# Convolving in full 128-row chunks through a DRAM scratch, with VectorE transposes in place of TensorE ones, in a convolution with two MLP layers

## The chip, the cores and the metric

The kernel runs on one core of a Trainium2 chip. The metric is the device time of one execution in microseconds (us). The core's engines are TensorE (PE for its matmuls, PEld for its weight loads), VectorE (DVE), ScalarE (ACT), GpSimd (POOL) and SyncE (SP), which here only issues DMAs. Each engine takes its instructions in program order and waits at the first one whose inputs are not ready.

## The reference, cut to what matters

```
w = softmax(weight, axis=-1)                      # 8 heads x 7 taps
x_pad = concat([zeros(B, 6, 192), x], axis=1)     # x: 2 x 4096 x 192, float32
y[b, s, h*24+g] = sum_k w[h, k] * x_pad[b, s+k, h*24+g]
y = y.reshape(8192, 192)
h = y @ moe_w_in                                  # 192 -> 2048
z = maximum(0.01*h, h) @ moe_w_out                # 2048 -> 192
h = z @ moe2_w_in                                 # 192 -> 2048
P = a0 + a1*h + a2*h^2 + a3*h^3
Q = 1 + |b0|*|h| + |b1|*h^2
out = (P / (Q + 1e-6)) @ moe2_w_out               # 2048 -> 192
```

## The kernel before

The 8192 tokens are cut into 16 blocks of 512. For each block, `prep` makes the convolved x in transposed form (channels on the partitions, 512 tokens along the row), `layer1` runs the first MLP over 16 tiles of 128 hidden units, `middle` splits its result for the next layer, `layer2` runs the second MLP over 16 tiles, and `finish` transposes and stores the result. Every factor is split into a high part of reduced precision and the rest, so a tile costs five 512-column matmuls in `gemm1` and five in `gemm2_hi` and `gemm2_lo`.

`prep` has these steps. `load_x` brings 512 tokens and their six predecessors into `xt` as five overlapping chunks of 109 rows. `conv` is, for each of two halves m of the channels, four matmuls of a banded matrix with the five chunks, each of 103 rows out and 120 columns; in float32 one such matmul leaves two records in the trace. `conv_evac` (ScalarE) copies the bank into `xc`, with a second copy of the last 64 channels for half 1. `trans` turns the chunks with five TensorE transposes for each half, the tokens put into the bank from the far end; `x_hi` (ScalarE) and `x_lo` (VectorE) then read the bank backwards and write `xh` and `xl`, from which `gemm1` reads. All banks that `conv`, `trans` and `gemm1` write come from one pool of four.

The order is written out by a planner. Each group of instructions has a rank, which is the due time of its tile (`t1` for layer 1, `t2` for layer 2) plus an offset for its kind (`OFF`). The planner goes through a modelled time and gives each engine the group that could start soonest, with a small pull (`PULL`) towards low ranks, among the `LOOK` lowest ranks within `WINDOW` of the lowest one left. `LEAD` is how long layer 1 runs alone at the start, `GAP` and `REST` set how far layer 2 follows behind, `STEP` is the planned time of a pair of tiles. A group with two engines named goes to the one that would end sooner. The buffers `work` (13, later 19, of 128x512 float32), `pair` and the banks are handed out in the same pass. Blocks 0 and 1 take turns in layer 1 while the weights still arrive and are split; from there on a block's layer 1 runs beside layer 2 of the block two before it. Before the first convolution, `s_warm` runs 13 matmuls that nothing reads.

Of the kernel before, what the change touches and what calls it, by code (L numbers as in the profile page):

```python
# [28 lines left out]
LOOK = 38  # L29
REST = 4.152  # L30
OFF = {'xfin_add': -25.96, 'xfin_main': -7.7, 'l2_rs': -12.47, 'l2_Q': -48.45, 'l2_lo': 22.42, 'cv_clip': 21.92, 'r_lo': 27.46, 'gemm2_lo': -13.68, 'fin_trans': 97.39, 'cv_abs': -48.47, 'gemm2_hi': -0.01, 'l2_R': -19.09, 'cv_low': -1.23, 'fin_evac': -37.98, 'trans': -11.11, 'mid_swap': -3.6, 'x_hi': 19.65, 'conv': -13.63, 'l2_p3': 0.9, 'r_hi': -31.67, 'x_lo': -0.75, 'fin_rest': -14.96, 'l2_abs': 32.4, 'l2_r': -7.07, 'l1_lo': -12.51, 'l2_D': -21.65, 'cv_bits': 22.1, 'l2_hi': -11.32, 'mid_add': -16.39, 'gemm1': -7.21, 'w_lo': -3.25, 'fin_add': -37.65}
TAIL = 0.239
FIN = 3.219
CV1, CV2, CV3 = 4.19, 18.33, 7.456
EVERY, INPLACE = 2, (1,)
N_WORK = 13
# [135 lines left out]
def conv_leaky_rational_kernel(  # L172
# [295 lines left out]
    def trans(eng, i, m):
        n = blocks[i][2]
# [433 lines left out]
```

## Time and profile before

| what | value |
|---|---|
| median of 3 runs | 1262.86 us (1261.99 to 1263.27) |
| the profiled execution | 1263.62 us |
| its span, first to last instruction | 1261.8 us |
| PE busy | 1235.6 us, 98% |
| ACT busy | 1145.2 us, 91% |
| DVE busy | 1100.1 us, 87% |
| POOL busy | 1033.2 us, 82% |
| mean granted TensorE clock | 0.993 |

Some 1.8 us of the execution lie outside the span. The profiled execution is 0.76 us above the median. The busy time of PE counts each matmul from its start to its modelled end, and matmuls overlap, so a busy PE is measured by how often a new matmul starts and not by its busy share alone.

### The profile page before, as it was taken

To read this page: it belongs to the slowest core of one execution; us is meant where nothing else is said; L and a number is where in the kernel's file an instruction comes from. 1 tells how busy PE (TensorE), PEld (TensorE's weight loads), DVE (VectorE), ACT (ScalarE), POOL (GpSimd) and SP (SyncE) were. 2 spreads that over 40 slices of the span, in tenths; PEclk is the share of its full clock that TensorE was granted. 3 is DMA by queue.
4 is the path that set the end of the run, shared out by engine and by line. 5 is a ranking of instruction groups with operands and counts; after the bars stand their busy time and mean duration, and the time that the engine had idled before them with its cause. 6 is when DMAs were issued, how large, how long until landed. Compare 5 with 4: busy or idle time off the path is not lost.

```text
span 1261.8 us, 17670 instructions
## 1 busy us (share of the span) xinstructions
PE 1235.6 (98%) x5584; PEld 1011.9 (80%) x5584; DVE 1100.1 (87%) x1661; ACT 1145.2 (91%) x2006; POOL 1033.2 (82%) x987
## 2 busy tenths in 40 slices
PE   8999999999999999999999999999999999999986
PEld 6887888888888788888888888888888888888764
DVE  6998989897987979889798888988888889889998
ACT  6999999999998989999898989989999999999996
POOL 2876878888797887969888888887888878788897
PEclk9999999999999999999999999999999999999989
DMA  7650001010000101010010101001010000000000
GB/s 216 181 157 7 1 1 29 1 28 1 14 15 1 28 1 29 1 29 1 1 29 1 29 1 28 1 1 28 1 29 1 13 1 1 13 1 13 1 13 14
DMA packets 70235, 30.25 MB, mean 24 GB/s; under 512 B 52566, under 2 KB 67580, under 8 KB 70140
## 3 DMA queue, kind: packets, MB, share of 16 engines
q1 hardware_dynamic: 68524, 28.91, 9.2%
q8 instruction: 44, 0.72, 0.2%
q14 instruction: 51, 0.42, 0.1%
q10 hardware_dynamic: 1616, 0.21, 0.1%
HBM read 20.70 MB, written 6.30 MB: 21 GB/s over the span
## 4 chain that ended last, share of the span: by engine, by line
PE 84%; ACT 8%; DVE 6%; issue 2%; DMA 1%; POOL 0%; SPq 0%; DVEq 0%; ACTq 0%; POOLq 0%
PE bank L249 43%; PE acc L249 40%; ACT work L240 4%; ACT raw L240 2%; DVE work L246 1%; PE bank L474 1%; DVE xl L243 1%; DVE pair L246 1%; DVE raw L246 1%; DVE bank L246 1%; DVE work L243 1%; DMA xt<-in_x_dram 1%; DVE raw L243 0%; ACT xh L240 0%; DVE pair L243 0%
## 5 line engine op out<-in xcount | busy, mean ns | idle before, releaser
L249 PE MATMUL acc<-pair,wo 128*128 128x512 f32 x2560 | 645.5, 392 | 2.5 <-DVE pair L243 1.2
L249 PEld LDWEIGHTS acc<-pair,wo 128*128 128x128 f32 x2560 | 478.1, 188 | 103.1 <-DVE pair L243 2.3
L240 ACT ACTIVATE work<-work 128x512 f32<-128x512 f32 x512 | 317.9, 630 | 21.4 <-DVE work L246 15.3
L243 POOL TENSOR_TENSOR work<-work,pair 128x512 f32<-128x512 f32 x181 | 234.7, 1298 | 54.3 <-DVE pair L246 49.5
L249 PE MATMUL bank<-xh,wiH 128*128 128x512 f32 x512 | 205.6, 402 | 14.7 <-DVE work L246 10.5
L249 PE MATMUL bank<-xl,wiR 128*128 128x512 f32 x512 | 200.6, 392 | 0.7 <-DVE xl L243 0.7
L249 PE MATMUL bank<-xh,wiL 128*128 128x512 f32 x512 | 200.6, 392 | 0.1
L249 PE MATMUL bank<-xl,wiH 128*128 128x512 f32 x512 | 200.5, 392 | 0.0
L249 PE MATMUL bank<-xh,wiR 128*128 128x512 f32 x512 | 200.4, 391 | 0.0
L243 POOL TENSOR_TENSOR pair<-work,work 128x512 fp32r<-128x512 f32 x122 | 157.8, 1296 | 25.9 <-DVE work L246 10.6
L246 DVE SCALAR_TENSOR_TENSOR work<-work,b_sb,bank 128x512 f32<-128x512 f32 x178 | 132.0, 741 | 45.2 <-ACT work L240 44.1
L246 DVE SCALAR_TENSOR_TENSOR pair<-bank,a_sb,work 128x512 fp32r<-128x512 f32 x177 | 131.4, 745 | 25.7 <-PE acc L249 15.5
L243 POOL TENSOR_TENSOR pair<-work,pair 128x512 fp32r<-128x512 f32 x96 | 125.4, 1307 | 32.0 <-PE acc L249 23.6
L240 ACT ACTIVATE work<-bank,a_sb 128x512 f32<-128x512 f32 x168 | 129.7, 772 | 19.0 <-PE bank L249 17.9
L246 DVE SCALAR_TENSOR_TENSOR work<-bank,a_sb,work 128x512 f32<-128x512 f32 x181 | 134.4, 743 | 12.5 <-POOL work L243 12.0
L249 PEld LDWEIGHTS bank<-xh,wiH 128*128 128x128 f32 x512 | 96.4, 188 | 47.2 <-DVE work L246 17.3
L246 DVE SCALAR_TENSOR_TENSOR bank<-work,a_sb,bank 128x512 f32<-128x512 f32 x168 | 125.4, 749 | 2.2
L240 ACT ACTIVATE raw<-raw 128x512 f32<-128x512 f32 x192 | 119.9, 630 | 8.0 <-DVE raw L246 5.9
L240 ACT ACTIVATE work<-bank,b_sb 128x512 f32<-128x512 f32 x178 | 121.4, 682 | 0.0
L249 PEld LDWEIGHTS bank<-xl,wiR 128*128 128x128 f32 x512 | 96.7, 189 | 21.6 <-DVE xl L243 1.1
L243 DVE TENSOR_TENSOR work<-work,bank 128x512 f32<-128x512 f32 x168 | 113.6, 677 | 0.0
L249 PEld LDWEIGHTS bank<-xl,wiH 128*128 128x128 f32 x512 | 96.7, 189 | 20.8 <-DVE xl L243 0.2
(96 smaller groups left out, 2002.2 us busy)
## 6 DMA issues: line engine op xcount, KB each, us to landing
raw<-in_moe_w_out_dram SPq DMA_DIRECT2D x16, 384.0 KB
xt<-in_x_dram SPq DMA_DIRECT2D x14, 384.0 KB
out_dram<-work SPq DMA_DIRECT2D x67, 64.0 KB
raw<-in_moe_w_in_dram SPq DMA_DIRECT2D x8, 512.0 KB
raw<-in_moe_w_in_dram SPq DMA_DIRECT2D x8, 256.0 KB
work<-work SPq DMA_DIRECT2D x16, 128.0 KB
out_dram<-raw SPq DMA_DIRECT2D x26, 64.0 KB
xt<-in_x_dram SPq DMA_DIRECT2D x18, 72.0 KB
```

The costliest lines, as they stand in the source:

```text
L240: nc.scalar.activation(out=out_, in_=in_, func=func, **k)
L243: (eng or nc.vector).tensor_tensor(out=out_, in0=in0, in1=in1, op=op)
L246: nc.vector.scalar_tensor_tensor(out=out_, in0=in0, scalar=s, in1=in1, op0=op0, op1=op1)
L249: nc.tensor.matmul(out=out_, lhsT=w, rhs=r, start=start, stop=stop)
L474: nc.tensor.transpose(ps[:, c1 - k:c1], xc[0:k, t, m * P:(m + 1) * P], ident[0:k, 0:k])
```

## The change

Blocks 0 and 1 stay as they are. For the other 14 blocks the convolution no longer goes block by block. The tokens from 1024 on are cut into chunks of 122 rows out of 128 rows in, 26 for the rest of the first sequence and 34 for the second, and these are put into 13 groups of four or five chunks. For each group, `load_g` loads one chunk per DMA, `conv_g` convolves it, `evac_g` copies the bank to `xc` without the extra 64 channels, and `put_g` writes the rows to a scratch tensor `y_dram` in DRAM, in token order from the far end, with two DMAs for a full chunk (112 and 10 rows).

For each block, `get_y` then reads the scratch back in eight DMAs of 64 KB (four for each half m), each in runs of 32 channels (128 bytes), so that 32x32 squares lie side by side in a `work` buffer, and `turn_y` transposes the squares on VectorE. `y_hi` (ScalarE or GpSimd) and `y_lo` (GpSimd or VectorE) split the result, now read from SBUF and not from a bank. The warm-up is 8 of the old matmuls and 19 short ones on a buffer that VectorE fills (`s_seed`). The planner's constants are new, among them the offsets in `OFF`.

```
-LEAD = 81.083
-GAP = 10.083
-PREP = 12.338
-WARM = 13
+LEAD = 66.057
+GAP = 6.373
+PREP = 56.276
+AHEAD = 40.0
+WARM = 8
+SHAPES = ((192, 6, 1), (384, 3, 1), (512, 3, 1), (256, 3, 1), (192, 4, 0))
...
-STEP = 4.683
-PULL = 0.003
-WINDOW = 94.713
-LOOK = 38
-REST = 4.152
+STEP = 4.016
+PULL = 0.005
+WINDOW = 193.974
+LOOK = 58
+REST = -0.364
...
-TAIL = 0.239
+TAIL = 5.502
-CV1, CV2, CV3 = 4.19, 18.33, 7.456
+CV1, CV2, CV3 = -20.785, 58.237, 26.634
...
+    CG = P - (K - 1)
...
-    xc = const.tile([CT, NTC, D + R], F32, name="xc")
+    xc = const.tile([CG, NTC, D + R], F32, name="xc")
+    y_dram = nc.dram_tensor("y_dram", (B * S, D), F32, kind="Internal").ap()
...
+    DIRECT = 2
+    groups = []
+    for bi in range(B):
+        t0 = max(blocks[DIRECT][3] - bi * S, 0) if bi == 0 else 0
+        count = -(-(S - t0) // CG)
+        starts = [min(t0 + c * CG, S - CG) for c in range(count)]
+        ng = -(-count // NTC)
+        at = 0
+        for g in range(ng):
+            k = min(NTC, -(-(count - at) // (ng - g)))
+            groups.append((bi, starts[at:at + k], t0 + at * CG))
+            at += k
...
+        t = xh[1][0][0]
+        for cols, count, step in SHAPES:
+            for n in range(count):
+                k = n * step % 4
+                mm(acc[0][1][:, 0:cols], t[:, k * P:(k + 1) * P], t[:, 0:cols], True, True)
...
+    def conv_g(eng, g, m):
+        k = len(groups[g][1])
+        pv = buf[("gps", g, m)][0:CG, 0:k * HC].rearrange("p (t c) -> p t c", t=k)
+        for hh in range(HB):
+            h = m * HB + hh
+            mm(pv[:, :, hh * G:(hh + 1) * G], band[:, h, P - CG:P], xt[g % 2][:, 0:k, h * G:(h + 1) * G], True, True)
...
+        act(xc[:, 0:k, m * HC:(m + 1) * HC], pv, ACTF.Copy)
...
+    def put_g(eng, g):
+        bi, starts, t0 = groups[g]
+        for c, s0 in enumerate(starts):
+            rows = s0 + CG - (t0 + c * CG)
+            r0 = B * S - bi * S - s0 - CG
+            even = rows - rows % 16
+            for a, z in ((0, even), (even, rows)):
+                if z > a:
+                    nc.sync.dma_start(out=y_dram[r0 + a:r0 + z, :], in_=xc[a:z, c, 0:D])
+
+    def get_y(eng, i, m):
+        n, tok0 = blocks[i][2:4]
+        r0 = B * S - tok0 - n
+        for d in range(1 + m):
+            for q in range((P, R)[m] // 32):
+                p0 = 32 * q + R * d
+                src = y_dram[r0:r0 + n, m * P + 32 * q:m * P + 32 * (q + 1)].rearrange("(b r) c -> r b c", r=32)
+                dst = buf[("ym", i, m)][p0:p0 + 32, 0:n].rearrange("r (b c) -> r b c", c=32)
...
+                    nc.sync.dma_start(out=dst, in_=src)
+
+    def turn_y(eng, i, m):
+        n = blocks[i][2]
+        nc.vector.transpose(out=buf[("yt", i, m)][:, 0:n], in_=buf[("ym", i, m)][:, 0:n])
...
+    def group(g):
...
+        on(SP(P * k * D * 4, k), max(base - 50, 8), 2.0, load_g, g, w=[xk], extra=DMA_LAND)
+        for m in range(2):
+            gps = ("gps", g, m)
+            on(PE(HB * 2 * (0.0025 + k * G / 1200.0)), base, 2.0 + 0.01 * m, conv_g, g, m, r=[xk, ("band", m)], w=[gps],
+               take=("bank", gps))
+            on(ACT(t_act(k * HC)), base, 4.0 + 0.01 * m, evac_g, g, m, r=[gps], w=[("xc", m)])
+        on(SP(0, k), base, 6.0, put_g, g, r=[("xc", 0), ("xc", 1), ("xc", 2)], w=[("y", g)], extra=DMA_LAND)
+
+    def fetch(i):
+        n, tok0 = blocks[i][2:4]
+        base = t1[i * NJ] - AHEAD
...
+            on(SP(0, 4), base, 12.0 + m, get_y, i, m, r=yk, w=[ym], take=("work", ym), extra=DMA_LAND + 1.0)
+            on(DVE(t_dve(n)), base, 18.0 + m, turn_y, i, m, r=[ym], w=[yt], take=("work", yt))
...
+            on(ACT(t_act(n, True)) + POOL(t_pool1(n)), base, 20.0 + m, y_hi, i, m, src, r=[yt], w=[("xh", 0, m, p)])
+            on(POOL(t_pool(n)) + DVE(1.2), base, 22.0 + m, y_lo, i, m, src, r=[yt, ("xh", 0, m, p)], w=[("xl", 0, m, p)])
...
     def prep(i):
+        if i >= DIRECT:
+            while made[0] < len(groups) and groups[made[0]][0] * S + groups[made[0]][2] < blocks[i][3] + blocks[i][2]:
+                group(made[0])
+                made[0] += 1
+            fetch(i)
+            return
```

## Rows read from the trace of the kernel before

**Rows 1.** Windows: stretch, us, then busy PE, PEld, DVE, ACT, POOL (instructions), clock, DMA, GB/s

```profile
160.00:1160.00 1000.00, 997.91 (x4559) 823.45 (x4558) 872.90 (x1304) 919.83 (x1604) 837.73 (x786) 1.00 0.05 12
...
1160.00:1261.80 101.80, 83.50 (x326) 63.02 (x324) 92.39 (x138) 87.55 (x148) 84.78 (x77) 0.93 0.05 9
```

**Rows 2.** Waits of PE in 160 to 1160 us, the longest: total us, times, longest

```profile
PE bank L249 <- ACT work L240: 0.8, 2, 0.5
```

**Rows 3.** The chain that ended last, one long piece: start us, length us

```profile
199.28 4.53 PE acc L249 x20
```

**Rows 4.** Groups by line and shape: busy us, mean ns, idle before

```profile
L249 PE MATMUL acc<-pair,wo 128*128 128x512 f32 x2560 | 645.5, 392 | 2.5 <-DVE pair L243 1.2 <-POOL pair L243 1.0
L249 PE MATMUL bank<-xl,wiH 128*128 128x512 f32 x512 | 200.5, 392 | 0.0
L249 PE MATMUL bank<-xt,band 109*103 109x120 f32 x256 | 32.2, 270 | 0.2 <-DMA xt<-in_x_dram 0.2
L474 PE MATMUL bank<-ident,xc 103*128 103x103 f32 x128 | 16.7, 253 | 0.2 <-ACT xc L240 0.2
```

**Rows 5.** Timeline of PE around one `conv` and one `trans`: start us, length us

```profile
1085.20 0.98 PE L249 MATMUL bank<-xt,band 109*103 109x120 f32 x8
1085.94 0.48 PE L249 MATMUL bank<-xh,wiH 128*128 128x512 f32 x1
1086.26 0.39 PE L249 MATMUL bank<-xh,wiL 128*128 128x512 f32 x1
...
1099.39 0.61 PE L474 MATMUL bank<-ident,xc 103*128 103x103 f32 x5
1099.78 1.40 PE L249 MATMUL acc<-pair,wo 128*128 128x512 f32 x5
1101.01 0.39 PE L249 MATMUL bank<-xh,wiH 128*128 128x512 f32 x1
```

**Rows 6.** Groups by line and shape, the other engines' steps of `prep` and their kin

```profile
L240 ACT ACTIVATE xh<-bank 128x512 fp32r<-128x512 f32 x32 | 18.9, 595 | 0.2 <-PE bank L474 0.2
L240 ACT ACTIVATE xc<-bank 103x480 f32<-103x480 f32 x32 | 18.1, 566 | 3.8 <-PE bank L249 3.7
L240 ACT ACTIVATE xc<-bank 103x320 f32<-103x320 f32 x15 | 6.5, 435 | 0.0
L527 POOL TENSOR_SCALAR pair<-work 128x512 fp32r<-128x512 f32 x69 | 44.1, 640 | 20.6 <-ACT work L240 12.9 <-PE acc L249 5.2 <-DVE bank L372 2.3
L243 POOL TENSOR_TENSOR pair<-work,pair 128x512 fp32r<-128x512 f32 x96 | 125.4, 1307 | 32.0 <-PE acc L249 23.6 <-ACT pair L240 1.8 <-DVE work L243 1.5
```

**Rows 7.** VectorE's work on `xl` by source: ns min/median/max, first and last start

```profile
L243 DVE TENSOR_TENSOR xl<-bank,xh x32: 672/680/692, 14.7 to 1105.5; 128x512 fp32r<-128x512 f32 x32
...
L243 DVE TENSOR_TENSOR xl<-work,xh x9: 679/881/1469, 99.6 to 1119.8; 128x512 fp32r<-128x512 f32 x9
L243 DVE TENSOR_TENSOR xl<-raw,xh x7: 692/1476/1785, 257.9 to 1193.1; 128x512 fp32r<-128x512 f32 x7
```

**Rows 8.** The SBUF-to-SBUF transposes of `finish`: ns min/median/max

```profile
L628 DVE STREAM_TRANSPOSE work<-work x9: 659/693/704, 194.8 to 1257.7; 64x512 f32<-64x512 f32 x9
```

**Rows 9.** SP's issues of the 64 KB output stores: ns min/median/max

```profile
L636 SPq DMA_DIRECT2D out_dram<-work x67: 315/488/1806, 193.7 to 1258.5; - x67
```

**Rows 10.** Windows of 1 us: six such stores, then a load of x

```profile
268.00:269.00 1.00, 1.00 (x7) 0.81 (x6) 0.95 (x2) 1.00 (x3) 1.00 (x3) 1.00 0.62 109
...
273.00:274.00 1.00, 1.00 (x6) 0.80 (x6) 1.00 (x3) 0.52 (x1) 0.91 (x1) 1.00 0.77 253
```

**Rows 11.** Timeline of PE at the start

```profile
2.40 8.51 PE L249 MATMUL acc<-qc,ident 128*128 128x256 f32 x26 [2.40 <-POOL ident masks.py:199]
10.74 1.81 PE L249 MATMUL bank<-xt,band 109*103 109x120 f32 x16
```

**Rows 12.** One window of 40 us in the steady stretch

```profile
320.00:360.00 40.00, 39.51 (x178) 32.45 (x177) 37.97 (x58) 38.60 (x67) 32.31 (x31) 1.00 0.10 23
```

**Rows 13.** Waits of PE over the whole span: total us, times, longest

```profile
PE bank L249 <- DVE work L246: 10.5, 10, 3.1
```

More of the change, by code (lines that the diff above doesn't have):

```diff
@@ L19 @@
 SIZES = [512] * 16
-LEAD = 81.083
-GAP = 10.083
-PREP = 12.338
-WARM = 13
+LEAD = 66.057
[4 more added lines that the diff above has]
+SHAPES = ((192, 6, 1), (384, 3, 1), (512, 3, 1), (256, 3, 1), (192, 4, 0))
 WIDE = 256
 FILL = {'conv': 1, 'trans': 1}
-STEP = 4.683
-PULL = 0.003
-WINDOW = 94.713
-LOOK = 38
-REST = 4.152
-OFF = {'xfin_add': -25.96, 'xfin_main': -7.7, 'l2_rs': -12.47, 'l2_Q': -48.45, 'l2_lo': 22.42, 'cv_clip': 21.92, 'r_lo': 27.46, 'gemm2_lo': -13.68, 'fin_trans': 97.39, 'cv_abs': -48.47, 'gemm2_hi': -0.01, 'l2_R': -19.09, 'cv_low': -1.23, 'fin_evac': -37.98, 'trans': -11.11, 'mid_swap': -3.6, 'x_hi': 19.65, 'conv': -13.63, 'l2_p3': 0.9, 'r_hi': -31.67, 'x_lo': -0.75, 'fin_rest': -14.96, 'l2_abs': 32.4, 'l2_r': -7.07, 'l1_lo': -12.51, 'l2_D': -21.65, 'cv_bits': 22.1, 'l2_hi': -11.32, 'mid_add': -16.39, 'gemm1': -7.21, 'w_lo': -3.25, 'fin_add': -37.65}
-TAIL = 0.239
+STEP = 4.016
[3 more added lines that the diff above has]
+REST = -0.364
+OFF = {'xfin_add': 27.93, 'xfin_main': -41.19, 'l2_rs': -6.51, 'l2_Q': -76.54, 'l2_lo': 20.05, 'cv_clip': 21.93, 'r_lo': -1.28, 'gemm2_lo': -4.32, 'fin_trans': 100.9, 'cv_abs': -25.96, 'gemm2_hi': -3.11, 'l2_R': -14.71, 'cv_low': -5.24, 'fin_evac': -75.01, 'trans': -38.96, 'mid_swap': -4.79, 'x_hi': 22.32, 'conv': -29.75, 'l2_p3': 3.44, 'r_hi': 17.48, 'x_lo': 2.67, 'fin_rest': -19.55, 'l2_abs': 22.74, 'l2_r': 2.84, 'l1_lo': -25.06, 'l2_D': -10.01, 'cv_bits': -8.15, 'l2_hi': -1.95, 'mid_add': -112.83, 'gemm1': -4.61, 'w_lo': -48.12, 'fin_add': -69.89, 'load_g': 63.41, 'conv_g': -23.42, 'evac_g': -35.87, 'put_g': 12.36, 'get_y': -27.55, 'turn_y': 19.29, 'y_hi': -15.46, 'y_lo': -20.59}
+TAIL = 5.502
 FIN = 3.219
-CV1, CV2, CV3 = 4.19, 18.33, 7.456
+CV1, CV2, CV3 = -20.785, 58.237, 26.634
 EVERY, INPLACE = 2, (1,)
@@ L336, in s_warm, with s_seed @@
             mm(acc[0][1][:, 0:WIDE], ident, qc[:, 0:WIDE], True, True)
+        t = xh[1][0][0]
[3 more added lines that the diff above has]
+                mm(acc[0][1][:, 0:cols], t[:, k * P:(k + 1) * P], t[:, 0:cols], True, True)
+    def s_seed(eng):
+        nc.vector.tensor_copy(out=xh[1][0][0], in_=qc)
     def s_fill(eng, count):
@@ L442, in zero_x, with load_g, zero_g, evac_g @@
         nc.vector.memset(xt[i % 2][0:K - 1, 0, :], 0.0)
+    def load_g(eng, g):
+        bi, starts, _ = groups[g]
+        t = xt[g % 2]
+        for c, s0 in enumerate(starts):
+            if s0 == 0:
+                load_rows(t, K - 1, c, x[bi, 0:CG, :], CG)
+            else:
+                nc.sync.dma_start(out=t[:, c, :], in_=x[bi, s0 - (K - 1):s0 + CG, :])
+    def zero_g(eng, g):
+        nc.vector.memset(xt[g % 2][0:K - 1, 0, :], 0.0)
+    def conv_g(eng, g, m):
[4 more added lines that the diff above has]
+            mm(pv[:, :, hh * G:(hh + 1) * G], band[:, h, P - CG:P], xt[g % 2][:, 0:k, h * G:(h + 1) * G], True, True)
+    def evac_g(eng, g, m):
+        k = len(groups[g][1])
+        pv = buf[("gps", g, m)][0:CG, 0:k * HC].rearrange("p (t c) -> p t c", t=k)
+        act(xc[:, 0:k, m * HC:(m + 1) * HC], pv, ACTF.Copy)
+    def put_g(eng, g):
+        bi, starts, t0 = groups[g]
+        for c, s0 in enumerate(starts):
+            rows = s0 + CG - (t0 + c * CG)
[12 more added lines that the diff above has]
+                dst = buf[("ym", i, m)][p0:p0 + 32, 0:n].rearrange("r (b c) -> r b c", c=32)
+                with nc.allow_non_contiguous_dma("columns of the convolution"):
+                    nc.sync.dma_start(out=dst, in_=src)
+    def turn_y(eng, i, m):
+        n = blocks[i][2]
+        nc.vector.transpose(out=buf[("yt", i, m)][:, 0:n], in_=buf[("ym", i, m)][:, 0:n])
     def conv_view(t, n):
@@ L459, in conv_evac @@
         ntc = -(-n // CT)
-        act(xc[:, 0:ntc, m * HC:(m + 1) * HC], pv, ACTF.Copy)
+        act(xc[0:CT, 0:ntc, m * HC:(m + 1) * HC], pv, ACTF.Copy)
         if m == 1 and i:
-            act(xc[:, 0:ntc, D:D + R], pv[:, :, HC - R:HC], ACTF.Copy)
+            act(xc[0:CT, 0:ntc, D:D + R], pv[:, :, HC - R:HC], ACTF.Copy)
     def conv_wrap(eng, i):
         pv = conv_view(buf[("cps", i, 1)], blocks[i][2])
-        nc.vector.tensor_copy(out=xc[:, 0:pv.shape[1], D:D + R], in_=pv[:, :, HC - R:HC])
+        nc.vector.tensor_copy(out=xc[0:CT, 0:pv.shape[1], D:D + R], in_=pv[:, :, HC - R:HC])
     def trans(eng, i, m):
@@ L477, in x_hi, with y_hi, y_lo @@
         n = blocks[i][2]
-        act(xh[l][m][i % 2][:, 0:n], src()[:, 0:n])
+        if eng == "POOL":
+            nc.gpsimd.tensor_scalar(out=xh[l][m][i % 2][:, 0:n], in0=src()[:, 0:n], scalar1=1.0, scalar2=0.0,
+                                    op0=ALU.mult, op1=ALU.add)
+        else:
+            act(xh[l][m][i % 2][:, 0:n], src()[:, 0:n])
     def x_lo(eng, l, i, m, src):
         n = blocks[i][2]
-        tt(xl[l][m][i % 2][:, 0:n], src()[:, 0:n], f(xh[l][m][i % 2][:, 0:n]), ALU.subtract)
+        tt(xl[l][m][i % 2][:, 0:n], src()[:, 0:n], f(xh[l][m][i % 2][:, 0:n]), ALU.subtract,
+           nc.gpsimd if eng == "POOL" else nc.vector)
+    def y_hi(eng, i, m, src):
+        x_hi(eng, 0, i, m, src)
+    def y_lo(eng, i, m, src):
+        x_lo(eng, 0, i, m, src)
     def gemm1(eng, l, i, j):
@@ L700, in conv_leaky_rational_kernel @@
     on(SP(0, 2), -60, 0, s_small, r=["tdram"], w=["ab"], extra=DMA_LAND)
-    on(PE(0.6 * WARM), -74, 0, s_warm, r=["ident", "qc"], w=[("acc", 0, 1)])
+    on(DVE(0.4), -83, 0, s_seed, r=["qc"], w=[("xh", 1, 0, 0)])
+    on(PE(0.6 * WARM + 2.2), -74, 0, s_warm, r=["ident", "qc", ("xh", 1, 0, 0)], w=[("acc", 0, 1)])
     on(ACT(0.2), -40, 0, s_abs, r=["ab"], w=["ab"])
@@ L731, in x_keys @@
         return [(t, l, m, i % 2) for t in ("xh", "xl") for m in range(2)]
-    def prep(i):
+    def group(g):
+        bi, starts, _ = groups[g]
+        k, p = len(starts), g % 2
+        first = next(i for i in range(NB) if blocks[i][3] + blocks[i][2] > bi * S + groups[g][2])
+        base = t1[first * NJ] - AHEAD
+        xk = ("xt", p)
+        if starts[0] == 0:
+            on(DVE(0.25), base - 50, 2.0, zero_g, g, w=[xk])
+        on(SP(P * k * D * 4, k), max(base - 50, 8), 2.0, load_g, g, w=[xk], extra=DMA_LAND)
[8 more added lines that the diff above has]
+        base = t1[i * NJ] - AHEAD
+        yk = [("y", g) for g, (bi, starts, t0) in enumerate(groups)
+              if bi * S + t0 < tok0 + n and bi * S + starts[-1] + CG > tok0]
+        for m in range(2):
+            ym, yt = ("ym", i, m), ("yt", i, m)
+            on(SP(0, 4), base, 12.0 + m, get_y, i, m, r=yk, w=[ym], take=("work", ym), extra=DMA_LAND + 1.0)
+            on(DVE(t_dve(n)), base, 18.0 + m, turn_y, i, m, r=[ym], w=[yt], take=("work", yt))
+            src = lambda k=yt, n=n: buf[k][:, 0:n][:, ::-1]
+            p = i % 2
+            on(ACT(t_act(n, True)) + POOL(t_pool1(n)), base, 20.0 + m, y_hi, i, m, src, r=[yt], w=[("xh", 0, m, p)])
+            on(POOL(t_pool(n)) + DVE(1.2), base, 22.0 + m, y_lo, i, m, src, r=[yt, ("xh", 0, m, p)], w=[("xl", 0, m, p)])
+    made = [0]
+    def prep(i):
+        if i >= DIRECT:
[4 more added lines that the diff above has]
+            return
         n = blocks[i][2]
```

## The prediction

> **What bounds the kernel now.** I read the busy windows first, then PE's waits, the chain, and the pace of single matmuls. In the stretch from 160 to 1160 us PE is busy for 997.91 of 1000 us, ACT for 919.8, DVE for 872.9, POOL for 837.7 [rows 1]. A busy PE can still be a stalled one, so the pace decides: 20 matmuls of 512 columns in a row take 4.53 us, 0.2265 us each [rows 3]. The program has 5120 of them: 2560 into `acc`, and five groups of 512 in `gemm1`, of which one is shown [rows 4]. That is 1159.7 us.
>
> A half of `conv` costs PE 0.834 us: its eight records start at 1085.20, the second matmul after them at 1086.26, and one matmul of 0.2265 lies between [rows 5]. A half of `trans` costs 0.488 us: from 1099.39 to 1101.01 there are 1.62 us, five large matmuls take 1.13 of them [rows 5]. So a block costs PE 320 x 0.2265 + 2 x 0.834 + 2 x 0.488 = 75.1 us, and 1000 us hold 13.3 blocks, or 4602 records at 346 a block. The window shows 4559 [rows 1]: PE runs there within 1% of its own pace, and its longest kind of wait sums to 0.8 us [rows 2]. In the middle, PE's work sets the time; the reader is to see that whatever is taken off PE there comes off the end, as long as the other three keep up.
>
> All of PE's work is 1159.7 + 16 x (1.67 + 0.98) = 1202.1 us. The other 59.7 us of the span of 1261.8 are the start, some stalls before 160 us, and the tail, where PE is busy for only 83.5 of 101.8 us while DVE has 92.4 [rows 1].
>
> **The change part by part, on PE.** Fourteen blocks lose `trans`: 28 x 0.488 = 13.7 us. They lose 28 halves of `conv`, 23.4 us, and 13 groups of two halves come in their place. Eight groups have five chunks, 120 columns as now; five have four, 96 columns. If columns count, this is 16 x 0.834 + 10 x 0.667 = 20.0 us, a saving of 3.4. But the band is now 122 columns wide and not 103, and if that width sets the pace, 26 x 0.834 x 122/103 = 25.7 us, a loss of 2.3. The columns that stream are nearest to what the row shows; I take a saving of 2.0 us, inside the two ends and short of the better one. PE in sum: 13.7 + 2.0 = 15.7 us less (11.4 to 17.1).
>
> **The other engines.** ScalarE loses 14 x (2 x 0.566 + 0.435 + 2 x 0.595) = 38.6 us and gains 26 copies of at most 0.566, 14.7 us [rows 6]. `y_hi` adds 28 x 0.64 = 17.9 us, on POOL at the price of its like [rows 6] or on ScalarE, for which I take the same. VectorE loses 28 x 0.68 = 19.0 us of `x_lo` [rows 7] and gains 28 transposes of 0.693 [rows 8], 19.4 us: even. `y_lo` reads two SBUF operands. On POOL its like takes 1.307 us [rows 6], 36.6 us in all; on VectorE the same operation with an SBUF source has medians of 0.881 and 1.476 where a bank as source has 0.680 [rows 7], so 25 to 41 us.
>
> By block, now: ScalarE 919.8/13.3 = 69.2 us, VectorE 65.6, POOL 63.0. Afterwards PE needs 75.1 - 15.7/14 = 74.0 us. With every choice against it, ScalarE has 68.8 us (93%), VectorE 68.6 (93%), POOL 66.9 (90%). In the window from 320 to 360 us PE lost 0.49 us with ScalarE at 96.5% and VectorE at 95% [rows 12]. So the three stay below the load at which PE was seen to wait, by a margin of a few per cent. I price them at nothing; the cover is PE's own work, and without it they cost what the second rival below says.
>
> **The DMAs.** SP issues per block eight fetches, and about nine pieces of `put_g` and four or five loads, where it had three loads; at 0.488 us an issue [rows 9] some 18 more issues are 9 us of a 74 us block. They are hidden as long as `get_y` is issued early (it waits for the landing of `put_g`, and behind it in SP's queue stand output stores, loads of x and, early on, weight pieces). Eight fetches move 512 KB in 128-byte runs. Output stores have such runs too and move 109 GB/s at 0.62 of the DMA engines, where a load of x reaches 253 [rows 10]: 4.7 us a block, of 74. The plan allows a half of `get_y` 2.4 us to issue and 3.3 us to land; four issues of 0.488 and 256 KB at 109 GB/s are 2.0 and 2.4 us. I price this at nothing; if it is late, `turn_y` stands at the head of VectorE's queue, behind it the layer 2 steps that give banks back, and then PE.
>
> A rule of the Trainium skill speaks against this part: "DMA: Bandwidth & Descriptors", Specifications, puts the least transfer for full rate at 512 bytes. The trace agrees in kind (109 against 253 GB/s [rows 10]). If all fetches lay open, 14 x 4.7 = 66 us would be added and the sum would be 1313 us; the third rival takes a part of it.
>
> A second one does: "VectorE: DVE Perf Modes", Rules for kernel authors, sends a 128x128 transpose to TensorE where PSUM will do as destination. Rows bear it out by the engine's own time, 0.488 us for a half on PE [rows 5] against 0.693 on VectorE [rows 8]. By it the old way stays, at 1262.9 us; by what bounds this stretch, PE's 0.488 is dear and VectorE's 0.693 is not.
>
> **Start, end and buffers.** The warm-up before was 8.51 us for 26 records, and the first `conv` stands right behind it, at 10.74 [rows 11]. The new one has 16 such records, 5.2 us, and 5376 columns, 2.4 us at 0.2265 for 512 or twice that at half the clock: 0.9 us less to 1.5 us more. I take nothing for it. Two banks a block are no longer taken for `trans`, four `work` buffers are taken instead: PE's waits for banks in the steady stretch are too small to gain from [rows 2], and I price the buffers with the second rival. The new constants move the start and the end; no row prices them, so I bound them by the tail: nothing to gain, or a part of its 18.3 us of idle PE [rows 1], or a loss of the same size. I take nothing.
>
> **Sum.** Profiled execution 1263.62 (span and 1.8 us around it) - 15.7 = 1247.9 us. It stands 0.76 us above the median of the runs, so 1247 us as a median.
>
> **The rivals.**
>
> 1. *The forecast*, PE's work comes off: 1247 us, by the bounds above 1243 to 1252.
>
> 2. *The elementwise engines take most of it back.* They get less time a block and a little more to do, and the `work` buffers are held through a fetch. If every 40 us of the new steady stretch, about 984 us, lost the 0.49 us of the dense window [rows 12], 24.6 x 0.49 = 12 us come back: 1259 us. For it: the window exists, and the two-operand steps on VectorE can take 1.476 us. Against it: ScalarE, the fullest, gets lighter.
>
> 3. *The fetch comes late* (the other side). The place is `turn_y` at the head of VectorE's queue, 28 times. PE's waits on VectorE are 1.05 us each in the mean over the whole span (10.5 in 10) [rows 13]. At that price, 28 x 1.05 = 29 us are added: 1276 us. It decides from 15.7/28 = 0.56 us a fetch that reaches PE. For it: `put_g` is planned at 0.6 us a chunk, but a chunk has two pieces of 0.488, so a group of five is some 1.9 us late on SP, with a wait for landing behind it. Against it: VectorE has (1000 - 872.9)/13.3 = 9.6 us of idle time a block to hide waits in, and the fetch ranks some 50 us ahead of the first tile.
>
> 4. *Start and end gain too.* The new `GAP`, `REST` and `STEP` leave less of layer 2 for the time after layer 1: (16 x 2.34 + 5.0 + 4.2)/37.5 = 1.25 blocks' worth by plan before, (16 x 2.008 + 3.2 - 0.4)/32.1 = 1.09 after. The tail has 18.3 us of idle PE [rows 1]; a third of it is 6 us, taken as an estimate: 1241 us. Against it: all 16 tiles of the last block's layer 2 still come after its layer 1, and VectorE is at 91% there.
>
> **How the numbers follow.** The forecast has 0.52, the second rival 0.17, the third 0.15, the fourth 0.16. The likeliest says 1247 us. The range reaches from 1237, a little below the fourth, to 1262, the second with its whole spread; what it leaves out is the third and a thin edge below. A measurement of this kernel tells about 0.2%, 2.5 us, from no change. Faster by more: the forecast, the fourth and most of the second, 0.80. Within: the rest of the second and the mildest of the third, 0.06. Slower by more: 0.14.
>
> **What the changed profile would show.** If right: no `bank<-ident,xc` matmuls past block 1; PE back to back in the middle, with 0.2265 us a matmul, a block in 74.0 us, the other three at 88 to 93%; waits of VectorE for a DMA into `work` short and without a follower on PE. Rival 2 shows as PE waits for banks spread over the middle, with two engines at 95% or more; rival 3 as idle time of VectorE ahead of `turn_y`, released by a DMA; rival 4 as a PE share above 83.5 in the last 102 us. I am wrong if PE's pace itself falls, or if the 13 wide convolutions cost more than 26 us.

## The result and the profile after

The changed kernel takes 1244.01 us (median of 4 runs, 1243.05 to 1246.15) where the one before takes 1263.07 (4 runs). The ratio is 0.9853 with a 95% interval of 0.9835 to 0.987: 1.5% faster, 3 us below the forecast of 1247 and inside its range. The profiled span is 1242.4 us, 19.4 less.

Windows of the changed kernel (columns as in [rows 1]):

```profile
160.00:1140.00 980.00, 979.83 (x4406) 811.73 (x4406) 879.32 (x1303) 913.65 (x1592) 863.76 (x802) 1.00 0.11 22
...
1140.60:1242.40 101.80, 83.54 (x328) 61.37 (x326) 89.46 (x134) 87.47 (x150) 81.72 (x72) 0.95 0.05 8
```

Against [rows 1], PE is as full as before in the middle, and the others are a little fuller: VectorE 89.7%, ScalarE 93.2%, GpSimd 88.1% of the 980 us. The last 101.8 us look as they did (PE 83.54, before 83.50). The gain is in the middle, and it does not show in a busy share. It shows in what PE's records are. The instructions on `xt` (the convolutions) in the changed kernel's middle (columns: PE, PEld, DVE, POOL, clock, DMA, GB/s):

```profile
160.00:1140.00 980.00, 21.84 (x176) 21.31 (x176) 0.22 (x1) 0.00 (x0) 1.00 0.11 22
```

The same of the kernel before, in 160 to 1160 us, and its instructions on `xc`, whose PE records are the transposes (columns here: PE, PEld, DVE, ACT):

```profile
160.00:1160.00 1000.00, 23.60 (x192) 22.77 (x192) 0.22 (x1) 0.00 (x0) 1.00 0.05 12
```

```profile
160.00:1160.00 1000.00, 15.80 (x130) 14.30 (x130) 0.00 (x0) 17.51 (x36) 1.00 0.05 12
```

So before, 4559 records were 192 of `conv`, 130 of `trans` and 4237 large matmuls; afterwards, 4406 are 176 of `conv_g` and 4230 large ones. What a half of `conv_g` costs is read from PE's timeline, with 120 columns and with 96:

```profile
643.88 1.01 PE L253 MATMUL bank<-xt,band 128*122 128x120 f32 x8
644.65 0.48 PE L253 MATMUL bank<-xh,wiH 128*128 128x512 f32 x1
644.97 0.39 PE L253 MATMUL bank<-xh,wiL 128*128 128x512 f32 x1
...
1025.77 0.99 PE L253 MATMUL bank<-xt,band 128*122 128x96 f32 x8
1026.54 0.94 PE L253 MATMUL acc<-pair,wo 128*128 128x512 f32 x3
1027.32 0.99 PE L253 MATMUL bank<-xt,band 128*122 128x96 f32 x8
```

With 120 columns it is 644.97 - 643.88 - 0.2265 = 0.86 us; with 96 it is 1027.32 - 1025.77 - 3 x 0.2265 = 0.87. The number of columns makes no difference here. With 0.865 us a half, the middle adds up: afterwards 4230 x 0.2265 + 22 x 0.865 = 977.1 of 980 us, 2.9 us of pauses; before 4237 x 0.2265 + 24 x 0.834 + 26 x 0.488 = 992.4 of 1000, 7.6 us of pauses. I use these pauses below as the measure of how well PE is fed; a pause inside a matmul's modelled length leaves PE "busy", and a stretch at a lower granted clock counts in them too.

The pauses can be seen in the profile as waits of the weight loads (PEld), which are not among the waits of PE's matmuls in [rows 2]. In the middle, in total, times and longest, they are for the kernel before (its three longest kinds), then for the changed one (its longest kind):

```profile
PEld bank L249 <- DVE pair L243: 3.0, 6, 0.9
PEld bank L249 <- ACT work L240: 2.6, 5, 0.9
PEld bank L249 <- DVE work L246: 2.2, 6, 0.7
```

```profile
PEld bank L253 <- DVE pair L247: 1.0, 2, 0.6
```

All kinds together are 8.8 us before and 3.2 us afterwards, near the pauses of 7.6 and 2.9.

The span's 19.4 us are then: `trans` gone, 13.7; `conv`, 28 x 0.834 - 26 x 0.865 = 0.9; fewer pauses in the middle, some 4.7. That is 19.3, so the start and the end together bring next to nothing. Each by itself agrees: up to 160 us PE began 568 large matmuls before and 570 now, and in the last 101.8 us it has 326 records before [rows 1] and 328 now.

The transposes by group (of the other groups, with a `raw` buffer as source or target, the mean is the same within 0.01 us), and GpSimd's part of `xl` (ns min/median/max, first and last start):

```profile
L515 DVE STREAM_TRANSPOSE work<-work 128x512 f32<-128x512 f32 x14 | 9.7, 696 | 0.0
```

```profile
L247 POOL TENSOR_TENSOR xl<-work,xh x14: 1274/1286/1305, 89.3 to 1070.1; 128x512 fp32r<-128x512 f32 x14
...
L247 POOL TENSOR_TENSOR xl<-raw,xh x11: 1271/1287/1305, 225.4 to 1052.0; 128x512 fp32r<-128x512 f32 x11
```

A VectorE transpose takes 0.70 us. The planner put 25 of the 28 `y_lo` on GpSimd at 1.29 us and 16 of the 28 `y_hi`.

The DMAs of one block, first SP's timeline, then VectorE's, then a window of 1 us while the fetch runs:

```profile
645.72 3.76 SPq L500 DMA_DIRECT2D y_dram<-xc  x10
649.66 4.04 SPq L511 DMA_DIRECT2D work<-y_dram  x8
```

```profile
660.02 0.70 DVE L515 STREAM_TRANSPOSE raw<-work 128x512 f32<-128x512 f32 x1
```

```profile
653.00:654.00 1.00, 1.00 (x6) 0.84 (x5) 0.97 (x2) 1.00 (x2) 1.00 (x1) 1.00 0.76 121
```

Ten writes take 3.76 us to issue, eight fetches 4.04; the fetch moves 121 GB/s at 0.76 of the DMA engines and is done by 655 us. The first of the two transposes comes 5 us later, and in this kernel VectorE never waits for a DMA into their source.

The start of PE's timeline (the short matmuls of the new warm-up, the first convolution, the first matmul of layer 1):

```profile
7.84 3.01 PE L253 MATMUL acc<-xh 128*128 128x192 f32 x19
12.22 2.09 PE L253 MATMUL bank<-xt,band 109*103 109x120 f32 x16 [1.36 <-DMA b_sb<-in_moe_b_dram]
...
17.83 0.58 PE L253 MATMUL bank<-xh,wiH 128*128 128x512 f32 x1
```

The convolution stood at 10.74 us before [rows 11] and is at 12.22 now, 1.36 us behind a DMA and not behind the warm-up, which ends at 10.85. The first matmul of layer 1 is at 17.83, where it was at 14.93 before; by 160 us, as counted above, that is made up.

### The profile page after: what moved, and what is told of

The parts are those of the page before. It is cut to its first block, busy times and chain, and to the rows that moved or that the text cites. A ratio compares the mean times of both kernels' runs of the same rounds, so it can differ in the third digit from the quotient of the medians.

```text
span 1242.4 us, 17891 instructions
## 1 busy us (share of the span) xinstructions
PE 1217.3 (98%) x5437; PEld 997.6 (80%) x5437; DVE 1112.0 (90%) x1671; ACT 1138.5 (92%) x1996; POOL 1059.2 (85%) x1000
## 4 chain that ended last, share of the span: by engine, by line
PE 81%; ACT 7%; DVE 7%; issue 2%; DMA 1%; POOL 1%; SPq 0%; POOLq 0%; DVEq 0%; ACTq 0%
PE bank L253 41%; PE acc L253 39%; ACT work L244 4%; DVE work L250 2%; ACT raw L244 1%; DMA raw<-in_moe_w_in_dram 1%; DVE bank L250 1%; DVE pair L247 1%; ACT bank L244 1%; DVE bank L396 1%; DVE bank L397 1%; DVE pair L250 1%; DVE work L247 0%; DVE raw L250 0%; POOL pair L247 0%
## 5 line engine op out<-in xcount | busy, mean ns | idle before, releaser
L253 PE MATMUL acc<-pair,wo 128*128 128x512 f32 x2560 | 657.4, 391 | 6.2 <-POOL pair L247 2.7
L244 ACT ACTIVATE work<-work 128x512 f32<-128x512 f32 x532 | 331.4, 630 | 17.6 <-DVE work L250 11.0
L247 POOL TENSOR_TENSOR work<-work,pair 128x512 f32<-128x512 f32 x184 | 239.5, 1302 | 43.6 <-DVE pair L250 34.6
L250 DVE SCALAR_TENSOR_TENSOR work<-work,b_sb,bank 128x512 f32<-128x512 f32 x182 | 135.1, 742 | 46.5 <-ACT work L244 45.3
L244 ACT ACTIVATE work<-bank,a_sb 128x512 f32<-128x512 f32 x176 | 135.3, 769 | 6.1 <-PE bank L253 6.0
L250 DVE SCALAR_TENSOR_TENSOR pair<-bank,a_sb,work 128x512 fp32r<-128x512 f32 x168 | 125.2, 745 | 13.1 <-ACT work L244 7.8
L250 DVE SCALAR_TENSOR_TENSOR bank<-work,a_sb,bank 128x512 f32<-128x512 f32 x176 | 132.1, 752 | 4.1
L244 ACT ACTIVATE raw<-raw 128x512 f32<-128x512 f32 x202 | 126.8, 630 | 6.2 <-DVE raw L250 3.6
L247 POOL TENSOR_TENSOR pair<-work,pair 128x512 fp32r<-128x512 f32 x92 | 120.3, 1308 | 7.0 <-PE acc L253 1.8
L247 DVE TENSOR_TENSOR work<-work,bank 128x512 f32<-128x512 f32 x176 | 119.3, 678 | 1.3 <-ACT raw L244 1.3
```

The lines of the kernel that those rows point to most:

```text
L250: nc.vector.scalar_tensor_tensor(out=out_, in0=in0, scalar=s, in1=in1, op0=op0, op1=op1)
```

## The experiments

The changed kernel and each experiment ran beside the kernel before on one chip, not the same chip for all, so I compare ratios; a ratio's difference to 0.9853, times 1262.5 us, is the distance to the changed kernel. Each ratio is known to about 0.0017, 2 us, so a difference of two of them to about 3 us. "Pauses" are those of 160 to 1140 us in the profiled execution, worked out as above from the counts of records. In seven of the profiled executions the clock granted in the first 30 us is 0.94 and not 1.00: the kernel before and the runs with VectorE transposes twice (with and without the planner told), the planner blind to the landing, all `y_lo` on VectorE, the old warm-up and the band of 64 columns. 0.06 of 30 us is 1.8 us, an estimate of what that costs ahead of the middle; it is in a distance and not in the pauses.

| run | ratio (95% interval) | distance to the changed kernel, us | pauses, us |
|---|---|---|---|
| changed kernel | 0.9853 (0.9835 to 0.987) | | 2.9 |
| PE transposes put back as dummies | 0.9928 (0.9911 to 0.9944) | +9.5 | 1.8 |
| VectorE transposes twice | 0.9944 (0.9929 to 0.9959) | +11.5 | 10.6 |
| VectorE transposes four times | 1.0343 (1.0327 to 1.0358) | +61.9 | 52 |
| twice, planner told | 0.9886 (0.9872 to 0.9901) | +4.2 | 5.1 |
| no VectorE transposes | 0.9866 (0.9852 to 0.9881) | +1.6 | 2.7 |
| planner blind to the landing | 0.9882 (0.9867 to 0.9896) | +3.7 | 5.1 |
| all `y_lo` on VectorE | 0.9878 (0.9863 to 0.9893) | +3.2 | 2.9 |
| old planner constants | 0.9914 (0.9899 to 0.9929) | +7.7 | 12.2 |
| kernel before, new constants | 1.0006 (0.9996 to 1.0015) | +19.3 | 7.6 |
| old warm-up | 0.9863 (0.9846 to 0.9879) | +1.3 | 2.7 |
| twelve groups | 0.9875 (0.9858 to 0.9891) | +2.8 | 5.5 |
| band of 64 columns | one run, 1248.98 us | +5.0 (to the median) | not worked out |

**Work put back on PE.**

```
     def conv_g(eng, g, m):
...
+        for t in range(5):
+            nc.tensor.transpose(buf[("gps", g, m)][:, t * CT:t * CT + 100], ident[0:100, :], ident[0:100, 0:100])
```

> The changed kernel with five TensorE transposes of the identity put ahead of each half of a group's convolution, into the same bank, which the convolution then overwrites: 130 transposes that nothing reads, in the same order of all else. Theory (PE's work sets the time): each set of five costs 0.488 us as in the kernel before, 26 x 0.488 = 12.7 us, so 1244.0 becomes 1256.7 us. Rival (the gain came from the new order of the planner or from the other engines): PE has room in the middle, and the time stays within 3 us of 1244.

The timeline of PE around one half in this run:

```profile
649.26 0.59 PE L484 MATMUL bank<-ident 100*128 100x100 f32 x5
649.69 1.03 PE L253 MATMUL bank<-xt,band 128*122 128x120 f32 x8
650.48 0.47 PE L253 MATMUL bank<-xh,wiH 128*128 128x512 f32 x1
650.80 0.39 PE L253 MATMUL bank<-xh,wiL 128*128 128x512 f32 x1
```

A set of five costs 650.80 - 649.26 - 0.2265 - 0.86 = 0.45 us here, 26 of them 11.7; 9.5 came out, and pauses fell by about 1 us. PE's work goes through to the end almost whole. The rival, room on PE, falls.

**Work added to VectorE, and taken off it.**

```
     def turn_y(eng, i, m):
         n = blocks[i][2]
-        nc.vector.transpose(out=buf[("yt", i, m)][:, 0:n], in_=buf[("ym", i, m)][:, 0:n])
+        for _ in range(2):
+            nc.vector.transpose(out=buf[("yt", i, m)][:, 0:n], in_=buf[("ym", i, m)][:, 0:n])
```

> The changed kernel with each VectorE transpose done twice in a row: 28 x 0.70 = 19.6 us more work on VectorE, 1.4 us a block, in the same order of all else. Theory (PE sets the time and VectorE has room, 89.7% busy in the middle): 1244 to 1246 us. Rival (VectorE is about to become the bound): up to 19 us more, 1263 us.

The second run is the same with `range(4)`:

> As before with four transposes in a row: 58.8 us more on VectorE, 4.2 us a block, which brings it to 95% of PE's 74 us a block. Theory: this is the load at which PE was seen to wait, so a part comes through, 5 to 20 us (1249 to 1264). Rival (VectorE is already the bound): all of it, 1300 us. Other rival (there is room for all of it): 1244 to 1246 us.

Both my theories fell: 11.5 us of 19.6, and 61.9 of 58.8. The middle of the two runs, one after the other:

```profile
160.00:1140.00 980.00, 975.94 (x4372) 803.84 (x4371) 885.36 (x1315) 908.71 (x1581) 857.13 (x794) 1.00 0.11 22
```

```profile
160.00:1140.00 980.00, 945.06 (x4189) 773.29 (x4188) 883.24 (x1307) 870.13 (x1514) 824.02 (x764) 0.99 0.11 21
```

VectorE is hardly busier than in the changed kernel (885 and 883 us against 879): its pace was not reached, it waits as before while PE falls behind. (With four transposes the granted clock is 0.99 in the stretch, so up to some 10 of the 52 us of pauses are a slower clock.) PE's weight loads with four transposes wait for VectorE in the middle, in total, times and longest:

```profile
PEld bank L253 <- DVE work L250: 26.7, 19, 4.1
PEld bank L253 <- DVE raw L250: 11.9, 8, 4.5
PEld bank L253 <- DVE pair L247: 7.0, 6, 2.6
```

These are single long waits for a bank, up to 4.5 us, a few for each block. That spoke for the place of the work and not for its amount, and two further runs tell these apart. First the doubled transpose with the planner told of it:

```
-            on(DVE(t_dve(n)), base, 18.0 + m, turn_y, i, m, r=[ym], w=[yt], take=("work", yt))
+            on(DVE(2 * t_dve(n)), base, 18.0 + m, turn_y, i, m, r=[ym], w=[yt], take=("work", yt))
```

> The changed kernel with each VectorE transpose done twice, as in the run that did so before, but with the planner told that a transpose takes twice as long, so that it places the rest of VectorE's work around it. That run was 11.5 us slower than the changed kernel. Theory (VectorE has the time, 89.7% busy in the middle, and what cost so much was 1.4 us unplanned at the head of its queue, with the layer 2 steps behind it that give banks back): 1244 to 1249 us. Rival (VectorE's total work sets the pace along with PE's): 1253 us or more.

Then no transpose at all, with `y_hi` and `y_lo` reading the fetched buffer (so the split is of squares that are not turned, and `ym` is held longer):

```
     def turn_y(eng, i, m):
         n = blocks[i][2]
-        nc.vector.transpose(out=buf[("yt", i, m)][:, 0:n], in_=buf[("ym", i, m)][:, 0:n])
+        pass
...
-            src = lambda k=yt, n=n: buf[k][:, 0:n][:, ::-1]
+            src = lambda k=ym, n=n: buf[k][:, 0:n][:, ::-1]
```

> The changed kernel without the VectorE transposes: the split reads the fetched buffer as it lies, so that the output is computed from blocks of x whose 32x32 squares are not turned; 28 x 0.70 = 19.6 us less work on VectorE. Theory (PE sets the time in the middle, and pauses are some 3 us there): 1240 to 1244 us. Rival (VectorE binds as much as PE): 1236 us or less.

The middle, with the planner told, then without transposes:

```profile
160.00:1140.00 980.00, 979.52 (x4396) 809.15 (x4395) 889.56 (x1324) 912.56 (x1587) 865.29 (x804) 1.00 0.11 22
```

```profile
160.00:1140.00 980.00, 979.83 (x4407) 811.89 (x4406) 866.91 (x1277) 913.35 (x1593) 863.75 (x802) 1.00 0.11 22
```

Planned for, the same 19.6 us cost 4.2 and not 11.5, and VectorE does more in the same time than in the changed kernel or in the two unplanned runs (889.56 us). The two orders differ as a whole, and an order can shift the time by a few us, but the 7.3 us between the runs are more than can be put down to that. Taken away, they bring nothing that can be measured: PE does 4407 records in the stretch, as in the changed kernel. So VectorE's amount of work does not bind, for up to 19.6 us more or less; four transposes with the planner told were not tried. What costs is work that the written order does not know of, at the head of a queue that otherwise runs close behind its plan.

**A fetch that comes late.**

```
-            on(SP(0, 4), base, 12.0 + m, get_y, i, m, r=yk, w=[ym], take=("work", ym), extra=DMA_LAND + 1.0)
+            on(SP(0, 4), base, 12.0 + m, get_y, i, m, r=yk, w=[ym], take=("work", ym), extra=0.0)
```

> The changed kernel with the planner told that a fetch from the scratch lands at the moment its last DMA is issued, in place of 3.3 us later; the waits themselves stay. VectorE's transposes are then put too early in its queue. Theory (VectorE has about 7.6 us of idle time a block that can take the wait, and little stands behind it): 1244 to 1248 us, with waits of VectorE for the DMA of up to 2 us each in the trace. Rival (a late fetch goes through to PE): 28 waits of 2 us, at half their length or more, 28 us and over: 1272 us.

VectorE's waits for the fetch over the whole span of this run:

```profile
DVE work L515 <- DMA raw<-y_dram: 2.6, 2, 2.2
...
DVE work L515 <- DMA work<-y_dram: 1.4, 1, 1.4
...
DVE raw L515 <- DMA work<-y_dram: 0.5, 1, 0.5
```

Four transposes waited, 4.5 us together; the other 24 had VectorE's queue ahead of them for long enough. Pauses rose by 2.2 us and the time by 3.7, just beyond what can be told; part of the 3.7 can be the clock at the start. The pauses come from the longest of the four, which ends at 199.19 us. Behind it PE's weight loads wait for VectorE twice, 0.71 us at 201.85 and then

```profile
205.80 0.19 PEld L253 LDWEIGHTS bank<-xh,wiH 128*128 128x128 f32 x1 [1.79 <-DVE pair L247]
```

and from 200 to 240 us PE begins 168 records where the changed kernel has 178, 2.3 us of work. So this late fetch went through to PE about one for one; but late fetches are rare even when the plan allows them no time.

**`y_lo` on VectorE alone.**

```
-            on(POOL(t_pool(n)) + DVE(1.2), base, 22.0 + m, y_lo, i, m, src, r=[yt, ("xh", 0, m, p)], w=[("xl", 0, m, p)])
+            on(DVE(1.2), base, 22.0 + m, y_lo, i, m, src, r=[yt, ("xh", 0, m, p)], w=[("xl", 0, m, p)])
```

> The changed kernel with all 28 y_lo on VectorE, where the planner put 25 of them on GpSimd. VectorE gets 25 x 0.7 to 1.5 us, 17 to 37 us, GpSimd loses 25 x 1.29 = 32 us. Theory (PE sets the time): 1243 to 1247 us, and the two-operand subtraction shows between 0.69 and 1.8 us each. Rival (the contention for operands with GpSimd slows VectorE enough for PE to wait): 1250 us or more.

```profile
L247 DVE TENSOR_TENSOR xl<-work,xh x29: 676/829/1680, 88.2 to 1178.8; 128x512 fp32r<-128x512 f32 x29
...
L247 DVE TENSOR_TENSOR xl<-raw,xh x15: 683/923/1773, 137.2 to 1032.0; 128x512 fp32r<-128x512 f32 x15
```

The two-operand subtraction (its rows by source above) takes from 0.68 to 1.77 us, as in [rows 7]. The planner knew of it, the middle keeps its pauses of 2.9 us, and the time is 3.2 us up, at the edge of what can be told. PE does not wait in the middle for this work; what is up lies elsewhere, and the clock at the start can be a part of it.

**The planner's constants by themselves.** The changed kernel with the old ones:

```
-LEAD = 66.057
-GAP = 6.373
+LEAD = 81.083
+GAP = 10.083
...
-WINDOW = 193.974
-LOOK = 58
-REST = -0.364
+WINDOW = 94.713
+LOOK = 38
+REST = 4.152
```

> The changed kernel with the planner's constants of the kernel before (LEAD, GAP, PREP, STEP, PULL, WINDOW, LOOK, REST, TAIL, CV1 to CV3 and the offsets of all kinds of work that both kernels have); the offsets of the new kinds, AHEAD and the warm-up stay new. Theory (14.6 us of the 19 are PE's work, the rest is the finer order): 1246 to 1251 us. Rival (the new constants make the gain): 1258 us or more.

and the kernel before with the new ones (the same lines the other way round):

> The kernel before with the planner's constants of the changed one (the same list without PREP and the offsets of conv and trans, which mean something else there). Theory: between 1257 and 1264 us, as PE's work is as before. Rival (the constants make the gain): 1250 us or less.

On the old structure the new constants change nothing (1.0006, pauses 7.6 us as before). On the new structure the old constants give 1251.2 us, 0.9914: that is 7.7 us short of the changed kernel, with 12.2 us of pauses in the middle and not 2.9. So the new work alone brings some 11 us of the 19, less than the 14.6 that PE has less to do, since the old order feeds PE worse there; the constants bring the rest, and only together with it.

Most of those 12.2 us stand in one place. The run with the new structure and the old constants, two matmuls with the wait ahead of each, then two windows:

```profile
177.87 0.97 PE L253 MATMUL acc<-pair,wo 128*128 128x512 f32 x3 [1.90 <-DVE pair L250]
180.44 0.80 PE L253 MATMUL bank<-xh,wiH 128*128 128x512 f32 x1 [1.61 <-DVE raw L250]
```

```profile
180.00:190.00 10.00, 9.56 (x30) 7.36 (x31) 8.18 (x13) 5.94 (x11) 8.44 (x8) 0.70 0.23 39
160.00:200.00 40.00, 36.49 (x156) 29.28 (x155) 31.52 (x47) 32.69 (x57) 31.63 (x30) 0.91 0.10 21
```

PE stops for 1.90 and 1.61 us behind VectorE, and then the granted clock is 0.70 in the mean of 10 us, so TensorE runs at its lower level (1.2 GHz) for a part of them. In these 40 us PE begins 156 records, the changed kernel 186: 30 x 0.2265 = 6.8 us. Outside this place the old constants leave 5.4 us of pauses, where the changed kernel has 2.9 in all. Which of the constants does it was not tried, nor whether the two banks a block that `trans` no longer takes have a part in it.

**The warm-up.** The changed kernel with 13 old matmuls and none of the short ones:

```
-WARM = 8
-SHAPES = ((192, 6, 1), (384, 3, 1), (512, 3, 1), (256, 3, 1), (192, 4, 0))
+WARM = 13
+SHAPES = ()
```

> The changed kernel with the old warm-up of 13 matmuls in place of 8 and 19 short ones; the planner's order may differ a little by the shorter planned time. Theory (the warm-up only has to fill the time until the band matrix has landed, some 12.2 us): 1243 to 1246 us. Rival (the short matmuls matter for the clock that TensorE is granted at the start): 1247 us or more, with a granted clock below 1.00 in the first 30 us.

1.3 us, within the uncertainty. The granted clock of the first 30 us is 0.94 in this run and 1.00 in the changed kernel; with the old warm-up before it was also 0.94. But the run in which the planner was blind to the landing has 0.94 too, with the new warm-up, and the kernel before with the new constants has 1.00 with the old one, so the warm-up does not settle it.

**Fewer groups, and a narrower band.** Twelve groups of five chunks, one of them across the two sequences:

```
+    chunks = []
+    for bi in range(B):
+        t0 = blocks[DIRECT][3] if bi == 0 else 0
+        for c in range(-(-(S - t0) // CG)):
+            chunks.append((bi, min(t0 + c * CG, S - CG), t0 + c * CG))
+    groups = [chunks[at:at + NTC] for at in range(0, len(chunks), NTC)]
```

> The changed kernel with 12 groups of five chunks in place of 13 of four or five; the sixth group takes its first chunk from the first sequence and four from the second. If a half of a group's convolution costs PE 0.865 us whatever its columns, one group less is worth 2 x 0.865 = 1.7 us: 1242.3 us. Rival (columns count): no work is saved, 1244 us. Or the new places in the planner's order cost more than that: 1246 us.

1246.3 us: 2.8 us more, not less, though within what can be told, with pauses of 5.5 us. The 1.7 us of PE's work are below what the order of all else shifts by.

```
-            mm(pv[:, :, hh * G:(hh + 1) * G], band[:, h, P - CG:P], xt[g % 2][:, 0:k, h * G:(h + 1) * G], True, True)
+            mm(pv[0:64, :, hh * G:(hh + 1) * G], band[:, h, P - CG:P - CG + 64], xt[g % 2][:, 0:k, h * G:(h + 1) * G], True, True)
```

> The changed kernel with a band matrix of 64 columns in place of 122 in the groups' convolution, so that only 64 of the 122 rows of each chunk are computed; all else is as in the changed kernel. In the changed kernel a half costs PE 0.86 to 0.87 us with 120 columns streamed and with 96 alike. Theory (the load of the weights, one for each of eight records, sets that pace, not the columns): a half with 96 columns falls to about 0.67 us and one with 120 to about 0.83. Rival (something fixed for each record does): both stay at 0.86. In sum 1 to 3 us off the time, too little to see in it.

PE's timeline in this run, with 120 columns and with 96:

```profile
647.59 1.03 PE L253 MATMUL bank<-xt,band 128*64 128x120 f32 x8
648.55 0.50 PE L253 MATMUL bank<-xh,wiH 128*128 128x512 f32 x1
648.89 0.39 PE L253 MATMUL bank<-xh,wiL 128*128 128x512 f32 x1
...
1030.86 0.87 PE L253 MATMUL bank<-xt,band 128*64 128x96 f32 x8
1031.66 0.96 PE L253 MATMUL acc<-pair,wo 128*128 128x512 f32 x3
1032.55 0.87 PE L253 MATMUL bank<-xt,band 128*64 128x96 f32 x8
```

A half that stands alone costs 648.89 - 647.59 - 0.2265 = 1.07 us with 120 columns and 1032.55 - 1030.86 - 0.68 = 1.01 with 96: more than with the full band. (The 1.07 leave out the matmul ahead, which starts 0.33 us before the first record and not 0.23; with it, 1.17.) But in some groups the two halves follow each other, and there the second half shows what eight records cost without a start and an end. PE's timeline with 96 and with 120 columns, in this run, then in the changed kernel:

```profile
184.72 1.53 PE L253 MATMUL bank<-xt,band 128*64 128x96 f32 x16
...
880.25 1.85 PE L253 MATMUL bank<-xt,band 128*64 128x120 f32 x16
```

```profile
182.73 1.85 PE L253 MATMUL bank<-xt,band 128*122 128x96 f32 x16
...
875.38 1.87 PE L253 MATMUL bank<-xt,band 128*122 128x120 f32 x16
```

Against the x8 rows above, eight more records take 1.53 - 0.87 = 0.66 us and 1.85 - 1.03 = 0.82 with the narrow band, in the ratio of their columns, and 1.85 - 0.99 = 0.86 and 1.87 - 1.01 = 0.86 with the full one. That is what the theory said (0.67 and 0.83): with 64 weight columns the columns that stream set the pace, with 122 the weights do. What the theory did not have is the cost of a set's start and end, about 0.34 us with the narrow band (1.01 - 0.66; 1.17 - 0.82) and 0.01 with the full one. PE's weight loads show the start of it, here, then in the changed kernel:

```profile
1030.85 0.69 PEld L253 LDWEIGHTS bank<-xt,band 128*64 128x64 f32 x8 [0.35 <-issue]
```

```profile
1025.54 1.06 PEld L253 LDWEIGHTS bank<-xt,band 128*122 128x122 f32 x8
```

Ahead of the first narrow load they stand idle for 0.35 us, for nothing that the profile shows; ahead of the full one they do not. Over the 24 halves after 100 us the sets cost 25.4 us in this run and 21.4 in the changed kernel, 4.0 us more work on PE. Its one time is 5.0 us above the changed kernel's median, which agrees, but one run with 0.94 at the start is no close test.

No version beat the changed kernel.

## Why the prediction was right, point by point

- *PE's work sets the time in the middle.* Right, and shown from both sides: 11.7 us of dummy transposes on PE cost 9.5 us, some 4 us of slower convolutions 5.0 us (one run), while 19.6 us less on VectorE brought nothing.
- *`trans`, 13.7 us.* Right: 0.488 us for a half before [rows 5], 0.45 for the dummies beside another neighbour.
- *`conv`, 2.0 us.* Too much: 0.9 us. I took the columns that stream for the nearest row; 96 columns cost as much as 120, and a half costs 0.865 and not 0.834. My other end, that the band's width sets the pace, was the right mechanism for the new convolutions, but I scaled 0.834 by 122/103 (0.988 a half, 25.7 us in all) as if the width had set the old pace too; 26 x 0.865 are 22.5. Inside the bounds I had set (3.4 to -2.3).
- *The other engines, priced at nothing.* Right in sum: 89.7, 93.2 and 88.1% against my 93, 93 and 90% at worst. But the reason given, a margin below 95%, was not the one that counts. With transposes doubled out of plan, VectorE was at 90% and PE lost 7.7 us more in the middle; with the same work in the plan it was at 91% and PE lost 2.2.
- *The DMAs, priced at nothing.* Right: 4.04 us for eight issues where I had 3.9, 121 GB/s where I had 109, done 5 us ahead of the transposes, no wait of VectorE for them. The low rate costs nothing here, since nobody waits. The trace agrees in the rate with what the Trainium skill says of pieces below 512 bytes ("DMA: Bandwidth & Descriptors", Specifications). For the transposes, 0.70 us on VectorE are cheaper here than 0.488 on PE. The Trainium skill's rule for a 128x128 transpose ("VectorE: DVE Perf Modes", Rules for kernel authors) would have kept the slower kernel.
- *The constants, priced at nothing.* This is the term that was off, by about 4 us, and it is why the time came out below 1247; that it came so near is in part luck, as `conv` was priced 1.1 us too high. My fourth rival expected such a gain at the start and the end. Neither brought it, and its sign, a PE share above 83.5 in the last 102 us, stands at 83.54. The gain lies in the middle, where pauses fell from 7.6 to 2.9 us, which I had called too small to gain from [rows 2]. The waits of PE's matmuls that I read there sum to 1.8 us in all. I did not read the waits of the weight loads, 8.8 us in the same stretch, though my own count of 4559 records for 4602 had room for them.
- *The second rival* (the other engines take it back) did not happen: 2.9 us of pauses in the middle, and no two engines at 95%. The run with old constants has 12.2 us, the size that I gave it, but not its signs: over half of them stand in one place, and VectorE and ScalarE are at 89.4 and 92.5% in the middle. *The third* (a late fetch) did not happen in the changed kernel; the blind planner made one such fetch, and it cost what it was late.

## What to carry to other kernels

Count what an engine's records are, not its busy share: two kernels with 100% busy TensorE differed by 5 us of pauses in 1000, and by the 13.7 us of transposes among the records. Read the waits of the weight loads beside those of the matmuls: here they held 8.8 us where the matmuls showed 1.8. Where one engine sets the pace, as here, a dearer operation on an engine with 10% to spare can be a gain, if the written order knows what it costs: unplanned, 19.6 us of work on VectorE cost 11.5 us, planned 4.2. A new structure and the constants of its order are one change; timed apart, they were worth 11 us and nothing.

## What was not expected of the hardware

A float32 matmul of 128 rows with 122 weight columns takes the same time for 96 columns streamed as for 120 (0.87 and 0.86 us for four of them, in eight records). With 64 weight columns, whose loads take 136 ns and not 186 in the mean, four further ones take 0.66 and 0.82 us, so there the columns that stream do count; but a set of four between matmuls with 128 weight columns takes 1.01 and 1.17, as its start and end cost about 0.34 us. With 103 weight columns, in the kernel before, four cost 0.834 us alone [rows 5], so neither the slower pace nor the dear start is seen there. Why the start of a set costs so much at 64 columns and next to nothing at 103 and 122 was not found.
